# A fused attention and bilinear-GLU block on one core: where the weight totals and the attention steps stand in the joint down projection of chunks 0 and 1

## The chip, the cores and the metric

The kernel runs on one core of one Trainium2 chip. The metric is the device time of one execution in microseconds (us); the median of the runs counts. The profile was taken from one such execution and has a span of 772.1 us, from the first instruction to the last.

The engines are named as the profile names them: PE is the matmul engine (PEld its weight loads), DVE the vector engine, ACT the scalar engine, POOL the general-purpose engine. SPq is the queue from which the sync engine issues most transfers. Each engine works through its own list of instructions in the order of the program; a semaphore makes it wait where an operand comes from another engine or from a transfer.

## What is computed

The input is 2048 rows of 1024 bf16 numbers. The block is a layernorm, a sliding-window attention, an output projection with a residual, a second layernorm, and a feed-forward part without a nonlinear function, again with a residual:

```python
h  = x + attention(layernorm(x), wqkv) @ wo        # 32 heads, 8 keys each, two rows apart
n  = layernorm(h)
h2 = h + ((n @ w_gate) * (n @ w_up)) @ w_down      # w_gate, w_up: 1024 x 3584, w_down: 3584 x 1024
```

The kernel works in four chunks of 512 rows. The change lies in one stage: the last product, `@ w_down`, of chunks 0 and 1 together.

## The kernel before

**The joint product.** The activations `g * u` of chunks 0 and 1 and the weight `w_down` are seen as 2 x 2 blocks: A11 and A12 are chunk 0 (even and odd blocks of 128 hidden features), A21 and A22 chunk 1; B11, B12, B21, B22 are the even and odd row blocks of `w_down`, left and right halves of its columns. Seven block products in place of eight give the four blocks of the result (a Strassen-Winograd scheme). It needs sums and differences of blocks, which are made in fp16. So activations and weights are first multiplied by a power of two each, taken from a bound: the sum of absolute values of every row, the total over all partitions, its exponent. `scale_h1` is the one for the activations, `scale_d` the one for the weights.

```python
class Scale:
    def add(self, k, src, junk):          # ACT: |src| summed along the row into column k of l1
        nc.scalar.activation(junk, src, ACTF.Abs, accum_out=self.l1[:, k:k + 1])
    def rows(self):                       # DVE: one number for each partition, and it in bf16
        nc.vector.tensor_reduce(row[:], self.l1[:], ..., ALU.add)      # profile: L639
        nc.vector.tensor_copy(self.rowb[:], row[:])                    # profile: L640
    def total(self, ps=None):             # PE sums over partitions, DVE makes the scales
        nc.tensor.matmul(ps[:, 0:n], lhsT=ones[:], rhs=self.rowb[:]...)  # profile: L645
        nc.vector.tensor_copy(tot[:], ps[:, 0:1])                      # L647
        ...                                # eb, eb, sb, ib: four DVE instructions on one column, L649 to L654
```

A product of the stage is 14 matmuls for each of four groups of 128 rows:

```python
def dprod(ps, q, lhs, rhs, fresh, lo=0, n=TC):
    for k in range(NP):                                                # NP = 14, profile: L944
        nc.tensor.matmul(ps[:, bass.ds(lo, n)], lhsT=lhs[k][:, bass.ts(q, 128)], rhs=..., ...)
```

**Loads and helpers.** `load_down` brings one half of a B block (two transfers of 896 KB); `load_h1` brings A21 or A22 back from device memory, to which chunk 1's activations were written (`hd1`), in two transfers of 1024 and 768 KB. `conv_h1`, `conv_down` and `conv_a` multiply a block by its power of two into fp16, on DVE unless ACT is named. `s1_half` is A21 + A22 for one half, `t_half(d, x, y, a)` is a difference of two B blocks for one half, `put` adds the residual to a finished result and stores it, `seed` copies one accumulator, scaled, into another (ACT). `pull(1)` issues the next step of the attention of chunk 3, which still runs on DVE meanwhile: an operation on 128 x 4096 elements or a pair of them.

**The stage.** Cut to the lines that matter:

```python
b12 = halves(((att, "qD"), (att, "kD")), "b12")
load_down(b12, 0, 1)
a21 = ...; a22 = ...
load_h1(a21, 0)
load_h1(a22, 1)
...
# output projection of chunk 2 on PE; ACT sums |B11| and |B21| beside it (abs_blocks, tiles junkb)
wo_adds(2, {0: in_turn(lambda: pull(1), lambda: abs_blocks(b11 + b21)), ...})
xs = four accumulators "ex";  ys = four accumulators "ey"

for q in range(4):
    dprod(xs[q], q, A11, cells_of(b11, NH), True)          # A11 B11, still in bf16
    if q == 0:
        conv_h1(a21, 0)
        conv_h1(a22, 0)
        s1_half(0)
        scale_d.rows()
    if q == 1:
        pull(1)
        conv_h1(a21, 1, nc.scalar)
        conv_h1(a22, 1, nc.scalar)
    if q == 2:
        scale_d.total(ys[3])
        inv1 = ...                                          # one DVE instruction
        for i in range(3):
            seed(i)                                         # ys[i] = xs[i] * scale_d.s
seed(3)
for q in range(4):
    ys[q] = ys[q] * scale_h1.s                              # ACT
pull(1)
s1_half(1)
b22 = ...; load_down(b22, 1, 1)
FS1 = A21 + A22
conv_a(A11, F11, 0, NP); conv_down(b22, nc.scalar)          # ACT
for q in range(4):
    dprod(xs[q], q, A12, cells_of(b21, NH), False)          # A12 B21 on top, still in bf16
    put(0, q, 0, ...)
    if q < 2:
        conv_down([b11[q], b12[q]])
    if q > 0:
        t_half(b11, b12, b11, q - 1) if q < 3 else None     # B12 - B11
conv_a(A12, F12, 0, NP)
...
for q in range(4):
    ev = ...
    dprod(ev, q, FS1, fcells(b11), True)                    # (A21 + A22)(B12 - B11)
    ...
    s_sums(F11, FS1, F11, ALU.subtract, ...)                # 14 small DVE differences in all
    if q > 1:
        t_half(t2, b22, b11, q - 2)                         # B22 - (B12 - B11)
pull(2)
...
for q in range(4):
    dprod(ys[q], q, F11, fcells(t2), False)
    ...
    s_sums(F12, F12, F11, ALU.subtract, ...)
    pull(1)
```

Of the kernel before, what the change touches and what calls it, by code (L numbers as in the profile page):

```python
# [78 lines left out]
def kernel(  # L79
# [11 lines left out]
    nc = tc.nc  # L91
# [565 lines left out]
    scale_gu, scale_d, scale_h = Scale("gu", 28), Scale("d", 23), Scale("h", 56)  # L657
# [125 lines left out]
    def put(c, t, hf, dst, ps, sc, other):  # L783
        nc.vector.scalar_tensor_tensor(dst, ps[:], sc, other, ALU.mult, ALU.add)
        nc.sync.dma_start(outf[bass.ds(c * TC + t * 128, 128), bass.ts(hf, 512)], dst)
# [132 lines left out]
    def f16(ap):  # L918
        return ap.bitcast(F16)

    def to_f16(dst, src, sc, eng=nc.vector):
        if eng is nc.scalar:
            nc.scalar.activation(dst, src, ACTF.Copy, scale=sc)
        else:
            eng.tensor_scalar(dst, src, sc, None, ALU.mult)

    def load_down(homes, e, hf):
        for a, t in enumerate(homes):
            nc.sync.dma_start(t[:, 0:NH, :], wd_e[e][:, bass.ts(a, NH), bass.ts(hf, 512)])

    def conv_down(homes, eng=nc.vector):
        for t in homes:
            to_f16(f16(t[:, 0:NH, :]), t[:, 0:NH, :], scale_d.s, eng)

    def sub(dst, x0, x1, eng=nc.vector):
        for d, a0, a1 in zip(dst, x0, x1):
            eng.tensor_tensor(f16(d[:, 0:NH, :]), f16(a0[:, 0:NH, :]), f16(a1[:, 0:NH, :]), ALU.subtract)
# [4 lines left out]
    def dprod(ps, q, lhs, rhs, fresh, lo=0, n=TC):  # L942
        for k in range(NP):
            nc.tensor.matmul(ps[:, bass.ds(lo, n)], lhsT=lhs[k][:, bass.ts(q, 128)], rhs=rhs[k][:, bass.ds(lo, n)],  # L944
                             start=(fresh and k == 0), stop=(k == NP - 1), skip_group_check=not fresh)
# [13 lines left out]
    def pull(n):  # L959
        for _ in range(n):  # L960
            next(atts[3], None)

    b11, b21 = ([wts["dn", n, a] for a in range(2)] for n in ("11", "21"))

    def halves(parts, name):
        return [pool.tile([128, KO, TC], BF, tag=tag, name=f"{name}{i}") for i, (pool, tag) in enumerate(parts)]

    b12 = halves(((att, "qD"), (att, "kD")), "b12")
    load_down(b12, 0, 1)
    a21 = halves(((lnTp, "lnT"), (lnTp, "lnT")), "a21")  # L970
    a22 = halves(((lnTp, "lnT"), (wpool, "w")), "a22")

    def load_h1(dst, e, parts=(0, 1)):
        for i in parts:
            t, k, n = ((dst[0], 0, 8), (dst[1], 8, 6))[i]
            nc.sync.dma_start(t[:, 0:n, :], hd1[:, 2 * k + e:2 * (k + n):2, :])

    load_h1(a21, 0)
    load_h1(a22, 1)
    state["live"] += 1  # L980

    def cells_of(homes, n=8):
        return [t[:, k, :] for t in homes for k in range(n)][0:NP]
# [55 lines left out]
    def s1_half(i):  # L1039
        n = (8, 6)[i]  # L1040
        s, t = (f16(a[i][:, 0:n, :]) for a in (a21, a22))
        nc.vector.tensor_tensor(s, s, t, ALU.add)

    def conv_h1(a, i, eng=nc.vector):
        n = (8, 6)[i]
        to_f16(f16(a[i][:, 0:n, :]), a[i][:, 0:n, :], scale_h1.s, eng)

    def t_half(dst, x0, x1, a):
        sub([dst[a]], [x0[a]], [x1[a]])

    def conv_a(cells, fcells_, lo, hi):
        for k in range(lo, hi):
            to_f16(fcells_[k], cells[k], scale_h1.s, nc.scalar)
# [12 lines left out]
    def seed(q):  # L1066
        nc.scalar.activation(ys[q][:], xs[q][:], ACTF.Copy, scale=scale_d.s)

    for q in range(4):
        dprod(xs[q], q, A11, cells_of(b11, NH), True)  # L1070
        if q == 0:
            conv_h1(a21, 0)
            conv_h1(a22, 0)
            s1_half(0)
            scale_d.rows()
        if q == 1:
            pull(1)
            conv_h1(a21, 1, nc.scalar)
            conv_h1(a22, 1, nc.scalar)
        if q == 2:  # L1080
            scale_d.total(ys[3])
            inv1 = const.tile([128, 1], F32, name="inv_h1d")
            nc.vector.tensor_tensor(inv1[:], scale_h1.inv, scale_d.inv, ALU.mult)
            inv1 = inv1[:]
            for i in range(3):
                seed(i)
    seed(3)
    for q in range(4):
        nc.scalar.activation(ys[q][:], ys[q][:], ACTF.Copy, scale=scale_h1.s)
    pull(1)  # L1090
    s1_half(1)
    b22 = halves(((lnTp, "lnT"), (wpool, "w")), "b22")
    load_down(b22, 1, 1)
# [3 lines left out]
    for q in range(4):  # L1097
        dprod(xs[q], q, A12, cells_of(b21, NH), False)
        put(0, q, 0, hs0[q][:, 0:512], xs[q], 1.0, hs0[q][:, 0:512])
        if q < 2:  # L1100
            conv_down([b11[q], b12[q]])
        if q > 0:
            t_half(b11, b12, b11, q - 1) if q < 3 else None
    conv_a(A12, F12, 0, NP)
    retire(4)
    hss[3] = load_x(3, "h", nc.sync)
# [34 lines left out]
    a22 = halves(((att, "vD"), (att, "oD")), "a22r")  # L1141
# [212 lines left out]
```

## Time and profile before

| What | Value |
|---|---|
| Time, median of 3 runs (lowest to highest) | 774.48 us (773.71 to 774.75) |
| Span of the profiled execution (its time) | 772.1 us (774.36 us) |
| PE busy over the span | 764.2 us, 99% |
| DVE, ACT, POOL busy | 79%, 66%, 18% |
| 412.00 to 424.50 us: PE, DVE, ACT busy, of 12.50 us | 9.62, 10.27, 11.32 us |
| 424.50 to 440.15 us: PE, DVE, ACT busy, of 15.65 us | 15.47, 15.31, 13.87 us |
| 440.15 to 452.20 us: PE, DVE, ACT busy, of 12.05 us | 12.05, 12.05, 12.05 us |
| 452.20 to 476.60 us: PE, DVE, ACT busy, of 24.40 us | 24.40, 18.53, 13.71 us |
| Granted clock of PE | 1.00 throughout these stretches |

The times inside the span count from its first instruction. The stage of the change begins at 412.38 us, with the first matmul of A11 B11. In a line of the timeline the columns are: start, busy time of the merged group, engine, line of the kernel, operation, written tile and read tiles, shapes, count, and in square brackets the idle time of the engine just ahead of it with what ended it. The view of waits gives, for a waiting engine and the one that ended its wait, the total, the number of times and the longest. The profile's ends of matmuls are modelled; starts are what to count with.

### The profile page before, as it was taken

The numbers are of one execution on the slowest core, as the hardware profiler recorded it, in microseconds if no ns is written. First come the engines' busy times: TensorE is split into PE (matmuls) and PEld (weight loads), VectorE is DVE, ScalarE is ACT, GpSimd is POOL, SyncE is SP. The second block draws the span as 40 slices with busy tenths as digits, with TensorE's granted clock in tenths as the row PEclk, the third lists the DMA queues.
The fourth block names the chain that finished last, engine by engine and source line by source line (L and its number), as shares of the span: only waits on it lengthen the run. The fifth ranks groups of instructions, "written<-read, shape, count | busy, mean of one in ns | idle before, by whom it ended". The sixth has DMA issues, their size and how long they took to land.

```text
span 772.1 us, 10299 instructions
## 1 busy us (share of the span) xinstructions
PE 764.2 (99%) x3663; PEld 351.1 (45%) x3663; DVE 606.2 (79%) x718; ACT 513.4 (66%) x979; POOL 141.9 (18%) x152
## 2 busy tenths in 40 slices
PE   9999999999999999999998999999999999999998
PEld 6444444444444444444443444444444444444444
DVE  5639999999899999999998996985553444568863
ACT  4638966423687398777899985836677676788240
POOL 0000000200002000020000001008778687600000
DMA  8999796999957699489568357774332423740001
GB/s 276 267 264 247 228 259 142 299 292 288 308 190 235 215 284 308 145 264 315 185 210 273 125 188 239 144 178 107 97 106 59 110 65 100 247 135 28 0 28 54
DMA packets 190915, 144.85 MB, mean 188 GB/s; under 512 B 81808, under 2 KB 181136, under 8 KB 188688
## 3 DMA queue, kind: packets, MB, share of 16 engines
q1 hardware_dynamic: 180416, 116.94, 53.9%
q0 software_dynamic: 3584, 22.02, 8.3%
q10 hardware_dynamic: 6864, 5.24, 2.5%
q8 instruction: 28, 0.46, 0.3%
q14 instruction: 23, 0.19, 0.1%
HBM read 110.10 MB, written 27.26 MB: 178 GB/s over the span
## 4 chain that ended last, share of the span: by engine, by line
PE 75%; DVE 15%; ACT 4%; issue 3%; DMA 3%; ACTq 0%; DVEq 0%; SPq 0%
PE ps L431 21%; PE dx L944 6%; PE py L826 6%; PE px L826 6%; PE pz L826 6%; PE pu L431 4%; PE pg L431 4%; PE pv L826 3%; PE ez L944 3%; PE ey L944 3%; DVE pv L523 3%; PE dy L944 3%; DVE prod L477 2%; PE wo L998 2%; PE wo L602 2%
## 5 line engine op out<-in xcount | busy, mean ns | idle before, releaser
L431 PE MATMUL ps<-lnT,w_qkv 128*128 128x512 bf16 x736 | 159.5, 379 | 0.0
L431 PEld LDWEIGHTS <-w_qkv 128*128 128x128 bf16 x736 | 71.9, 98 | 86.1
L344 ACT CAST sg<-ps 128x512 bf16<-128x512 f32 x96 | 55.3, 586 | 47.6 <-PE ps L431 40.8
L477 DVE TENSOR_TENSOR prod<-qD,kD 128x4096 bf16<-128x4096 bf16 x32 | 72.2, 2285 | 12.4 <-DMA kD<-kd 12.4
L523 DVE TENSOR_TENSOR pv<-vD,at 128x4096 bf16<-128x4096 bf16 x32 | 72.4, 2285 | 0.2
L826 PEld LDWEIGHTS <-sw 128*128 128x128 f16 x448 | 43.8, 98 | 52.9 <-issue 0.2
L431 PEld LDWEIGHTS <-w_wu 128*128 128x128 bf16 x448 | 43.8, 98 | 52.9
L431 PEld LDWEIGHTS <-w_wg 128*128 128x128 bf16 x448 | 43.8, 98 | 52.9
L826 PE MATMUL px<-lnT,ws 128*128 128x512 bf16 x224 | 55.2, 379 | 0.0
L536 POOL DMA_DIRECT2D od<-oD x4 | 2.2, 544 | 276.7 <-DVE oD L534 276.7
L431 PE MATMUL pg<-lnT,w_wg 128*128 128x512 bf16 x224 | 52.9, 379 | 0.0
L431 PE MATMUL pu<-lnT,w_wu 128*128 128x512 bf16 x224 | 52.9, 379 | 0.0
L431 PE MATMUL pwu<-lnT,w_wu 128*128 128x512 bf16 x224 | 52.9, 379 | 0.0
L431 PE MATMUL pwg<-lnT,w_wg 128*128 128x512 bf16 x224 | 52.9, 379 | 0.0
L826 PEld LDWEIGHTS <-ws 128*128 128x128 f16 x336 | 32.9, 98 | 39.7
L807 POOL TENSOR_TENSOR sw<-ws 128x512 f16<-128x512 f16 x26 | 30.0, 1155 | 85.5 <-PE pv L826 51.9
L944 PEld LDWEIGHTS <-gs 128*128 128x128 f16 (+1 forms) x280 | 27.4, 98 | 36.4 <-issue 3.6
L479 DVE TENSOR_TENSOR prod<-prod 128x4096 bf16<-128x4096 bf16 x16 | 36.6, 2289 | 0.4
L843 ACT COPY py<-px 128x512 f32<-128x512 f32 x28 | 16.0, 570 | 27.8 <-PE px L826 27.8
L808 POOL TENSOR_TENSOR sw<-sw,ws 128x512 f16<-128x512 f16 x26 | 30.0, 1155 | 2.0
L810 POOL TENSOR_TENSOR sw<-ws,sw 128x512 f16<-128x512 f16 x26 | 30.0, 1155 | 0.0
L809 POOL TENSOR_TENSOR sw<-ws 128x512 f16<-128x512 f16 x26 | 30.0, 1155 | 0.0
(334 smaller groups left out, 1474.8 us busy)
## 6 DMA issues: line engine op xcount, KB each, us to landing
w_wg<-in_B_w_gate_dram SPq DMA_DIRECT2D x14, 1024.0 KB, 6.9
w_wu<-in_B_w_up_dram SPq DMA_DIRECT2D x14, 1024.0 KB, 6.3
w_pair<-in_B_w_gate_dram SPq DMA_DIRECT2D x14, 512.0 KB, 4.0
w_pair<-in_B_w_up_dram SPq DMA_DIRECT2D x14, 512.0 KB, 5.3
w_wo<-in_A_wo_dram SPq DMA_DIRECT2D x6, 1024.0 KB, 7.2
w_qkv<-in_A_wqkv_dram SPq DMA_DIRECT2D x5, 1024.0 KB, 10.9
kd<-sg SPq DMA_DIRECT2D x32, 144.0 KB, 4.2
kD<-kd POOLq DMA_DIRECT2D x4, 1152.0 KB, 9.0
```

Of the source, the lines that this page charges most:

```text
L344: nc.scalar.copy(sg[:, HB:HB + TC], ps[:])
L431: nc.tensor.matmul(ps[:], lhsT=wt[:, ko, bass.ts(j, 128)], rhs=rhs[:, ko, :], start=(ko == 0), stop=(ko == KO - 1))
L477: nc.vector.tensor_tensor(prod[:, j], qD[:], kD[:, :, o:o + SUB], ALU.mult)
L479: nc.vector.tensor_tensor(prod[:, :, 0:16], prod[:, :, 0:16], prod[:, :, 16:32], ALU.add)
L523: nc.vector.tensor_tensor(pv[:, j], vD[:, :, o:o + SUB], at[:, w, None, :].to_broadcast((128, DH, SUB)), ALU.mult)
L807: eng.tensor_tensor(sw[:, i, 0], a21, a22, ALU.add)
L808: eng.tensor_tensor(sw[:, i, 1], sw[:, i, 0], a11, ALU.subtract)
L809: eng.tensor_tensor(sw[:, i, 2], a11, a21, ALU.subtract)
L810: eng.tensor_tensor(sw[:, i, 3], a12, sw[:, i, 1], ALU.subtract)
L826: nc.tensor.matmul(ps[:], lhsT=lhs[:, ko, :], rhs=rhs[:, ko, :], start=(fresh and ko == 0), stop=(ko == 3), skip_group_check=not fresh)
L843: nc.scalar.copy(yb[i][:], xb[i][:])
L944: nc.tensor.matmul(ps[:, bass.ds(lo, n)], lhsT=lhs[k][:, bass.ts(q, 128)], rhs=rhs[k][:, bass.ds(lo, n)], start=(fresh and k == 0), stop=( ...
```

## The change: what it does and what it is for

The sum over rows of the weight bound (`scale_d.rows`) was placed on DVE behind two conversions and a sum of the A blocks; it now stands behind the first conversion alone, so that the total over partitions, a matmul in the middle of A11 B11, finds its operand earlier. The rest fills DVE in another order: the sum `s1_half(0)` comes behind the total; the weight conversions stand in one block right behind it instead of between the products of A12 B21; each weight difference is one step earlier in that loop; two attention steps move from ahead of the weight work to behind it. On ACT the second conversion of A22 comes behind the first three seeds. On the transfer queue the loads of A21 and A22 go ahead of that of B12. No instruction is added or taken away.

```diff
     b12 = halves(((att, "qD"), (att, "kD")), "b12")
-    load_down(b12, 0, 1)
     ...
     load_h1(a21, 0)
     load_h1(a22, 1)
+    load_down(b12, 0, 1)
     ...
         dprod(xs[q], q, A11, cells_of(b11, NH), True)
         if q == 0:
             conv_h1(a21, 0)
+            scale_d.rows()
             conv_h1(a22, 0)
-            s1_half(0)
-            scale_d.rows()
         if q == 1:
-            pull(1)
             conv_h1(a21, 1, nc.scalar)
-            conv_h1(a22, 1, nc.scalar)
         if q == 2:
             scale_d.total(ys[3])
             ...
+            s1_half(0)
             for i in range(3):
                 seed(i)
+            conv_h1(a22, 1, nc.scalar)
     seed(3)
     for q in range(4):
         nc.scalar.activation(ys[q][:], ys[q][:], ACTF.Copy, scale=scale_h1.s)
-    pull(1)
+    for a in range(2):
+        conv_down([b11[a], b12[a]])
     s1_half(1)
     ...
         put(0, q, 0, hs0[q][:, 0:512], xs[q], 1.0, hs0[q][:, 0:512])
         if q < 2:
-            conv_down([b11[q], b12[q]])
-        if q > 0:
-            t_half(b11, b12, b11, q - 1) if q < 3 else None
+            t_half(b11, b12, b11, q)
+        else:
+            pull(1)
```

## The prediction, written before the result was known

> **What bounds the kernel now.** The first line of the page says which engine to look at.
>
> ```profile
> PE 764.2 (99%) x3663; PEld 351.1 (45%) x3663; DVE 606.2 (79%) x718; ACT 513.4 (66%) x979; POOL 141.9 (18%) x152
> ```
>
> PE has only 772.1 - 764.2 = 7.9 us without a matmul. A reorder that adds and removes nothing can gain only from those. The view of waits, for PE alone, names them:
>
> ```profile
> PE ey L645 <- DVE rowbd L640: 2.9, 1, 2.9
> PE warm_ps L338 <- DVE warm L324: 1.2, 1, 1.2
> PE ps L392 <- ACT lnT L387: 0.4, 1, 0.4
> PE ps L392 <- DMA w_qkv<-in_A_wqkv_dram: 0.3, 1, 0.3
> PE ex L944 <- ACT ey L1067: 0.2, 1, 0.2
> ```
>
> The first and the last are of the changed stage; the rest belong to the start. L645 is the matmul that totals the weight bound over partitions. The PE timeline shows it in place:
>
> ```profile
> 412.38 9.23 PE L944 MATMUL ex<-w_dn,gs 128*128 128x512 bf16 x42
> 424.49 0.38 PE L645 MATMUL ey<-rowbd,ones 128*128 128x512 bf16 x1 [2.88 <-DVE rowbd L640]
> 424.70 3.18 PE L944 MATMUL ex<-w_dn,gs 128*128 128x512 bf16 x14
> 428.07 12.25 PE L944 MATMUL ex<-w_dn,gs 128*128 128x512 bf16 x56 [0.18 <-ACT ey L1067]
> 440.15 12.25 PE L944 MATMUL ev<-w_dn,a 128*128 128x512 f16 x56
> ```
>
> From 428.07 to 440.15 there are 56 matmuls: 12.08 / 56 = 215.7 ns from start to start. So PE was free for the total at 412.38 + 42 x 0.2157 = 421.44 and got it at 424.49: 3.05 us lost. After it, 14 matmuls should end their slots at 424.70 + 3.02 = 427.72, but the next started at 428.07: 0.35 lost. Together 3.40 us. The DVE timeline says why `rowbd` came late:
>
> ```profile
> 417.12 1.27 DVE L925 TENSOR_SCALAR a<-a,sbh 128x4096 f16<-128x4096 bf16 x1
> 420.55 1.29 DVE L925 TENSOR_SCALAR a<-a,sbh 128x4096 f16<-128x4096 bf16 x1 [2.16 <-DMA a<-hd]
> 421.87 2.29 DVE L1042 TENSOR_TENSOR a<-a,a 128x4096 f16<-128x4096 f16 x1
> 424.08 0.17 DVE L639 TENSOR_REDUCE rowd<-l1d 128x1 f32<-128x23 f32 x1
> 424.28 0.16 DVE L640 CAST rowbd<-rowd 128x1 bf16<-128x1 f32 x1
> 424.35 2.28 DVE L534 TENSOR_TENSOR oD<-oD,pv 128x4096 bf16<-128x4096 bf16 x1
> 426.55 0.15 DVE L647 COPY totd<-ey 128x1 f32<-128x1 f32 x1
> 427.18 0.14 DVE L654 TENSOR_SCALAR ibd<-ebd 128x1 int32<-128x1 int32 x1
> 446.81 3.95 DVE L937 TENSOR_TENSOR t<-b,w_dn 128x3584 f16<-128x3584 f16 x2
> ```
>
> The two row operations stand behind two conversions and a sum, and the second conversion waits 2.16 us for A22. Then an attention step of 2.28 us (L534) stands ahead of the copy of the total, so the scale is ready only near 427.3, and the first seed starts at 427.36 (the 0.18 above). On ACT the last summing of |B21| ended at 418.80: the rows could have been had from then on.
>
> [...] the trace has 2.28 us against 1.28 for 4096 columns, so the moved sums and attention steps are the long pieces.
>
> **The change, part by part.** I follow the new order with the durations above; on DVE I count from start to start, as operations overlap slightly there.
>
> *Rows.* DVE: first conversion 417.12 to 418.39, rows after ACT's 418.80, so about 419.0, bf16 copy done at 419.3. PE needs it at 421.44: slack 2.1. This takes away the 3.05, wherever A22 lands.
>
> *Total and seeds.* The second A22 half stays on ACT, but behind three seeds. The second DVE conversion runs 419.3 to 420.6 if A22 is there. The total starts on PE at 421.44, ends near 421.85; copy to `inv1` takes 427.44 - 426.55 = 0.89, so until 422.75. Seed 0 runs about 422.6 to 423.3; PE wants that accumulator at 421.44 + 0.21 + 3.02 = 424.67. Slack 1.4, so the 0.35 goes too. Seed 3 comes behind the conversion (seeds to 424.4, conversion 2.86 to 427.2, seed to 427.8), but PE needs it only after three more groups, at 424.67 + 9.06 = 433.7.
>
> *Loads.* Bytes and queue are the same; A21 and A22 (3.67 MB) pass B12 (1.84 MB). Before, A22's halves landed at about 420.5 and 422.7 (the two waits on them), at the end of some 5.5 MB. Now about B12's share, an estimated 1.84 MB / 350 GB/s = 5 us, is taken off their wait (350 GB/s is what the DMA view shows in these us), and B12 is last, near 422.7. Its first use is now at 422.75 + 2.21 (A sum) + 1.06 = 426.0: slack 3.
>
> *DVE, the part to worry about.* Its work up to the last weight difference is the same, but PE comes 3.4 us earlier. Before, from 420.55 to 450.68 DVE had 30.13 us with 0.28 idle, so 29.85 of work. Of this, conversion, rows and scale (1.32 + 0.27 + 0.89) lie ahead of 422.75 now. What is left is 27.37: two A sums 2.21 + 1.67, four weight conversions 4.24, four differences 3.87 + 3.87, four puts 2.41, two attention steps 4.40, 14 small differences 4.70. Sum: 422.75 + 27.37 = 450.1. Its points against PE:
>
> First difference B12 - B11: 422.75 + 2.21 + 4.24 + 1.67 + 0.60 + 1.94 = 433.4; PE starts `ev` at 424.67 + 12.08 = 436.75. The second: 433.4 + 0.60 + 1.94 = 435.95 against 436.75 + 7 x 0.2157 = 438.3. Both have over 2 us, where before the second ended at 441.6 for a need of 441.66. This is what moving the attention steps is for.
>
> Then attention and puts to 441.55, small differences to 446.25, B22 - (B12 - B11): first half 448.2, second 450.1 to 450.2. PE ends `ev` at 436.75 + 12.09 = 448.84 and needs the second half at 448.84 + 1.51 = 450.35. Slack 0.6 and about 0.15: just in time, so an expected loss of 0.1, up to 1 if some DVE piece waits.
>
> *Further on.* Differences for A12 end some 0.6 earlier than before (461.5 for 462.1); the last is needed at 460.9 + 2.8 = 463.7. DVE had an idle 4.77 us after these, so its debt ends there. The last attention output ends at about 458.2 and its transfers some 13 us later (before: 458.75, landed by 472.4); PE wants it from 473.1 on, before from 476.41. Slack remains. From there each later step hangs on PE and shifts with it.
>
> Sum: 3.05 + 0.35 - 0.1 = 3.3 us. 774.48 - 3.3 = 771.2.
>
> **The rivals.**
>
> *DVE becomes the bound.* PE's wait would not vanish but move to the start of `ey`, on L937 (t). For it: from 424.5 to 452.2 DVE is busy 27.36 of 27.70 us, and by my count 0.15 us remains. Against it: DVE begins the scale 4.7 us earlier (421.86 for 426.55), as the 2.16 us wait is gone and two attention steps moved. If DVE loses 1 to 2 us to a wait that I don't see, the time is 772 to 773.
>
> *B12 lands too late.* It is now last in the queue. DVE would wait at its conversion, and through the tight chain each us would arrive at PE, less 0.15. For it: three of four A loads issue with long gaps, and A21's second half must wait for chunk 1's last store. Against it: 3 us of slack. At 2 us late it costs nothing; at 5 us late, 773.
>
> *The gain is absorbed later*, by something that doesn't move with PE: the way of chunk 3's attention through device memory. Its slack falls from some 4 us to some 1.3 (landed 471.8, last rows) or more, as the first rows are used first. If it were to fail, up to 3 us come back: 774.
>
> *Nothing to gain* would need the PE wait to be hidden. A wait on an engine that is 99% busy and on the chain is not; I give this little.
>
> **Range and chances.** Centre 771.2. Medians of three of the same kernel lie in 773.71 to 774.75, half a us each way. Below, no more than the 3.4 can come from this stage, so 770.3 is the end with noise. Above, I allow 1.3 us for the tight DVE chain and noise: 772.6. 2% of 774.48 is 15.5 us; PE's whole idle time is half of that, so "faster by over 2%" is all but excluded, and so is the reverse, as the order is only changed inside some 40 us with PE near full in both.
>
> **What would show it right or wrong.** Right: no PE wait on `rowbd`; the total at about 421.4 and A12 B21 at 424.7, `ev` at 436.8, `ey` at 448.8, the output projection of chunk 3 at 473.1; PE's busy time unchanged and the span near 768.8. The DVE conversion of A22 without a DMA wait; L937 of t ending within 0.3 us of 450.2. Wrong: a PE wait on L937 (t) at `ey`, or on L1112; a DVE wait on B12; a wait of the output projection on oT; or a later wait that takes back the 3.3 us.

## The result: 770.39 us for 774.62, and the profile after

The changed kernel takes 770.39 us (median of 6 runs, 770.02 to 770.98), the kernel before on the same chip 774.62 us (6 runs, 773.71 to 775.11). The ratio is 0.9948, with a 95% interval of 0.9935 to 0.9960: 4.2 us faster, inside 2%. The predicted time was 771.2 with a range of 770.3 to 772.6.

The waits of PE, changed kernel (who waited for whom, total, times, longest):

```profile
PE warm_ps L338 <- DVE warm L324: 1.2, 1, 1.2
PE pt L386 <- DVE ln L379: 0.8, 1, 0.8
PE ps L392 <- DMA w_qkv<-in_A_wqkv_dram: 0.5, 1, 0.5
PE ps L392 <- ACT lnT L387: 0.3, 1, 0.3
```

All four belong to the start of the kernel. The waits on `rowbd` and on the seed are gone and nothing took their place. The PE timeline, changed kernel:

```profile
412.41 9.23 PE L944 MATMUL ex<-w_dn,gs 128*128 128x512 bf16 x42
421.48 0.38 PE L645 MATMUL ey<-rowbd,ones 128*128 128x512 bf16 x1
421.69 15.27 PE L944 MATMUL ex<-w_dn,gs 128*128 128x512 bf16 x70
436.80 12.25 PE L944 MATMUL ev<-w_dn,a 128*128 128x512 f16 x56
448.89 12.25 PE L944 MATMUL ey<-t,gs 128*128 128x512 f16 x56
```

A11 B11 and A12 B21 have become one group of 70 without a gap. From the first matmul of `ex` to the first of `ey<-t` there are 42 + 1 + 14 + 56 + 56 = 169 slots; 169 x 0.2157 = 36.45 us, and the trace has 448.89 - 412.41 = 36.48. I call this span the stage length. It is now where PE alone would put it, with no wait left. In the kernel before it was 452.24 - 412.38 = 39.86, from the line of 412.38 in the prediction to this one of the same timeline:

```profile
452.24 12.25 PE L944 MATMUL ey<-t,gs 128*128 128x512 f16 x56
```

The DVE timeline, changed kernel, at the two places that mattered:

```profile
418.86 0.18 DVE L639 TENSOR_REDUCE rowd<-l1d 128x1 f32<-128x23 f32 x1 [0.43 <-ACT junkb L635]
419.15 1.28 DVE L925 TENSOR_SCALAR a<-a,sbh 128x4096 f16<-128x4096 bf16 x1
421.89 0.16 DVE L647 COPY totd<-ey 128x1 f32<-128x1 f32 x1 [1.46 <-PE ey L645]
446.27 3.95 DVE L937 TENSOR_TENSOR t<-b,w_dn 128x3584 f16<-128x3584 f16 x2
```

The row sums wait for nothing but the last sum on ACT; A22 is there when its conversion comes (no wait on the line at 419.15, where 2.16 us stood before); DVE now waits for PE, 1.46 us, in place of the reverse. The differences t end at 450.22, 0.18 us ahead of PE's need for the second half at 448.89 + 1.51 = 450.40.

The traces explain 772.1 - 768.7 = 3.4 us of span. The times differ by 4.2. The rest is settled below.

### The profile page after: what moved, and what is told of

It is laid out like the page before. It is cut to its first block, busy times and chain, and to the rows that moved or that the text cites. A ratio compares the mean times of both kernels' runs of the same rounds, so it can differ in the third digit from the quotient of the medians.

```text
span 768.7 us, 10302 instructions
## 1 busy us (share of the span) xinstructions
PE 762.8 (99%) x3663; PEld 350.7 (46%) x3663; DVE 606.0 (79%) x718; ACT 513.1 (67%) x979; POOL 142.5 (19%) x152
## 4 chain that ended last, share of the span: by engine, by line
PE 97%; DVE 2%; DMA 1%; issue 0%; ACTq 0%; DVEq 0%
PE ps L431 21%; PE dx L944 6%; PE pz L826 6%; PE pwu L431 6%; PE pu L431 6%; PE py L826 6%; PE pwg L431 6%; PE pg L431 6%; PE px L826 6%; PE wo L998 4%; PE pv L826 3%; PE ez L944 3%; PE ey L944 3%; PE ex L944 3%; PE dy L944 3%; PE wo L578 2%
```

## The experiments

Times are medians; each ratio is against the kernel before on the same chip, with its 95% interval, and is the recorded estimate, not the quotient of the medians shown. Not all rows ran on the same chip. The stage length is the sharper measure, as it is read inside one trace. Where a line of a trace has x41, x55 or x69, one record is missing: the starts fit 42, 56 and 70.

| Kernel | Stage length, us | Time, us | Ratio to before |
|---|---|---|---|
| before | 39.86 | 774.62 | |
| changed | 36.48 | 770.39 | 0.9948 (0.9935 to 0.9960) |
| row sums moved alone | 39.66 | 774.53 | 0.9996 (0.9986 to 1.0007) |
| row sums and total moved | 39.40 | 773.50 | 0.9987 (0.9980 to 0.9993) |
| the same, and ACT's conversion behind the seeds | 39.40 | 773.58 | 0.9986 (0.9977 to 0.9995) |
| changed, old loads | 36.47 | 770.61 | 0.9949 (0.9934 to 0.9964) |
| changed, row sums second | 36.47 | 770.63 | 0.9950 (0.9935 to 0.9964) |
| changed, both of these | 37.07 | 771.14 | 0.9951 (0.9939 to 0.9963) |
| changed, ACT's conversion ahead of the seeds | 36.66 | 770.90 | 0.9941 (0.9927 to 0.9955) |
| the same, old loads | 37.73 | 772.16 | 0.9956 (0.9942 to 0.9970) |
| changed, attention step later | 36.47 | 770.75 | 0.9954 (0.9939 to 0.9968) |
| changed, one DVE operation more | 37.88, and one more wait behind it | 772.76 | 0.9969 (0.9958 to 0.9980) |
| changed, again | 36.47 | 771.00 | 0.9948 (0.9937 to 0.9960) |

**Row sums moved alone**, the edit in the kernel before:

```diff
             conv_h1(a21, 0)
+            scale_d.rows()
             conv_h1(a22, 0)
             s1_half(0)
-            scale_d.rows()
```

> The kernel before with one edit: the row sums of the weight bound stand behind the first conversion of A21, as in the changed kernel; loads, attention steps and conversions stay. Theory 1 (a wait moves on): PE gets the total at about 421.5 us and loses nothing there, but the copy of the total still stands on DVE behind the A22 conversion (held by its load until 420.5), the A sum and an attention step, so the scale is ready at about 427.1 us; A12 B21 then waits some 3.1 us for the first seed and starts near 427.9 instead of 428.07. Gain 0.2 us, time same as before. Rival (the row sums are the gain, as the title of the change says): the 2.9 us wait just goes, gain about 3 us.

The PE timeline, row sums moved alone:

```profile
421.99 0.38 PE L645 MATMUL ey<-rowbd,ones 128*128 128x512 bf16 x1
422.20 3.19 PE L944 MATMUL ex<-w_dn,gs 128*128 128x512 bf16 x14
428.42 12.25 PE L944 MATMUL ex<-w_dn,gs 128*128 128x512 bf16 x55 [3.03 <-ACT ey L1067]
```

DVE took its operations in the order of the program both times: the row sums ran at 424.08 in the kernel before and at 419.36 here, ahead of the conversion that waits for A22 (420.55 and 421.16). The total runs without a wait, and one product later PE waits 3.03 us for the seed. The stage is 0.20 us shorter, as expected. A wait of 2.88 us on one line is not 2.88 us of gain: behind it stood a second wait with the same end.

**Row sums and total moved**: the A sum and the attention step that stood ahead of the total go behind it too.

```diff
             conv_h1(a21, 0)
+            scale_d.rows()
             conv_h1(a22, 0)
-            s1_half(0)
-            scale_d.rows()
         if q == 1:
-            pull(1)
             ...
             inv1 = inv1[:]
+            s1_half(0)
+            pull(1)
```

> The kernel before with the row sums moved forward and the A sum and the attention step that stood ahead of the total moved behind it; the attention steps stay ahead of the weight differences, and the loads stay in the old order. Theory 1: A12 B21 starts at 424.7 us (3.4 us gained), but the first weight difference ends at about 438.5 us where the next product wants it at 436.8 (wait 1.7), the second at 441.0 where it is wanted at 440.0 (wait 1.0): gain left 0.7 us. Rival (DVE has room enough for the attention steps where they were): gain 3.4 us.

The PE timeline, row sums and total moved:

```profile
425.88 12.25 PE L944 MATMUL ex<-w_dn,gs 128*128 128x512 bf16 x55 [1.19 <-ACT ey L1067]
438.51 1.67 PE L944 MATMUL ev<-w_dn,a 128*128 128x512 f16 x7 [0.39 <-DVE w_dn L937]
441.05 10.74 PE L944 MATMUL ev<-w_dn,a 128*128 128x512 f16 x49 [0.86 <-DVE w_dn L937]
```

The stage gains 0.46 us, where 0.7 was expected. The weight differences hold PE back, though by 1.3 us in all and not by 2.7, since the wait of 1.19 us for the seed, which was not foreseen, came ahead of them. Two runs follow it up.

**ACT's second A22 conversion put back ahead of the seeds**, in the changed kernel, with the new and with the old order of the loads:

```diff
             conv_h1(a21, 1, nc.scalar)
+            conv_h1(a22, 1, nc.scalar)
         ...
             for i in range(3):
                 seed(i)
-            conv_h1(a22, 1, nc.scalar)
```

> The changed kernel with ACT's second A22 conversion put back ahead of the seeds; loads in the new order. The run with row sums and total moved showed a wait of 1.2 us for the first seed that was not expected there, with that conversion ahead of the seeds and A22 loaded last. Theory 1 (the place of this conversion counts, and the more the later A22 lands): with A22 landed early ACT converts 421.5 to 424.35 us, the first seed ends at about 425.0, PE wants it at 424.7: wait 0.3 us, time 0.3 above the changed kernel. Rival (the conversion's place costs nothing): no wait.

> The same with the loads in the old order too. Theory 1: the conversion waits for its load until some 422.3 to 422.7 us and ends near 425.3, the first seed ends at 426.0, PE waits 1.2 to 1.5 us; time 1.2 to 1.5 above the changed kernel. So the order of the loads is worth 1 us here and nothing where the conversion stands behind the seeds. Rival (the wait came from DVE, as the scale was late): no wait here, as the scale is at 422.7 us.

The ACT timeline of the second, with old loads:

```profile
422.77 2.86 ACT L923 ACTIVATE a<-a,sbh 128x3072 f16<-128x3072 bf16 x1 [0.95 <-DMA a<-hd]
425.54 2.38 ACT L1067 ACTIVATE ey<-ex,sbd 128x512 f32<-128x512 f32 x4
```

The scale was ready at 423.0, but ACT held the seeds until 425.54, as the conversion ahead of them waited for A22. PE lost 1.25 us of stage length. With the new order of the loads the same placing costs 0.19 us (0.3 expected). So the early A22 load takes away all but 0.19 us of this wait, and the conversion behind the seeds takes away all of it, with either order of the loads.

**The attention steps and the weight conversions**: the run above with row sums and total moved, and in addition ACT's conversion behind three seeds. Against the changed kernel only the attention steps, the weight conversions with the differences behind them, and the loads stand as before. The edit in the changed kernel, without the loads:

```diff
             s1_half(0)
+            pull(1)
             for i in range(3):
                 seed(i)
     ...
-    for a in range(2):
-        conv_down([b11[a], b12[a]])
+    pull(1)
     s1_half(1)
     ...
         if q < 2:
-            t_half(b11, b12, b11, q)
-        else:
-            pull(1)
+            conv_down([b11[q], b12[q]])
+        if q > 0:
+            t_half(b11, b12, b11, q - 1) if q < 3 else None
```

> The run with row sums and total moved, with ACT's second A22 conversion behind three seeds: against the changed kernel only the attention steps and the weight conversions stand in their old order (and the loads, which the run with old loads showed to cost nothing). Theory 1: A12 B21 starts without a wait at 424.7 us, and all of the loss now stands at the weight differences: PE waits 1.7 us for the first and 0.9 to 1.0 for the second; time as in the run with the conversion ahead, to 0.2 us, since DVE set it there too; 2.6 us above the changed kernel. Rival (half the loss there was ACT's): 1.2 us faster than that run.

The PE timeline, attention ahead:

```profile
421.73 15.27 PE L944 MATMUL ex<-w_dn,gs 128*128 128x512 bf16 x69
438.74 1.67 PE L944 MATMUL ev<-w_dn,a 128*128 128x512 f16 x7 [1.74 <-DVE w_dn L937]
441.28 10.73 PE L944 MATMUL ev<-w_dn,a 128*128 128x512 f16 x49 [0.86 <-DVE w_dn L937]
```

No wait for the seed any more, and the stage is exactly as long as with it, 39.40 us: DVE's weight differences set the end in both. The old order of attention steps and conversions costs 39.40 - 36.48 = 2.92 us (2.6 expected), of the 3.38 that the whole change brings in this stage. This is the largest part. The two steps take 4.5 us on DVE here, 425.03 to 429.56, ahead of work that PE waits for. But the conversions were not tried alone, and the 2.92 belong to the pair: with the steps away and the conversions still between the products, DVE would be done with the A sum near 425.03 + 1.67 = 426.70 and could not take the first finished product before 421.73 + 2 x 3.02 = 427.77, an estimated idle time of 1 us where, as shown below, only some 0.2 us can be spared. What moving the steps would bring with the total still late is open too.

**Loads and row sums**, undone one at a time and together in the changed kernel.

```diff
+    load_down(b12, 0, 1)                  # old loads
     ...
-    load_down(b12, 0, 1)
     ...
-            scale_d.rows()                # row sums second
             conv_h1(a22, 0)
+            scale_d.rows()
```

> The changed kernel with the loads in the order of the kernel before (B12 ahead of A21 and A22). Theory 1 (the order of the loads is worth nothing while the row sums stand ahead of the A22 conversion): that conversion waits for its load until about 420.5 us and ends at 421.85, when the total arrives from PE (421.86 to 421.9): PE timeline as in the changed kernel to 0.1 us, same time. Rival (the early A22 is part of the gain): the total is late and PE waits 0.5 us or more, or the load of B22 and B12 shifts a DVE wait.

> The changed kernel with the row sums behind both DVE conversions. Theory 1 (with A22 loaded early the place of the row sums is worth nothing): the second conversion runs right behind the first, 418.4 to 419.6 us, the row sums are done at about 419.9, still 1.5 us ahead of PE's need at 421.5: no PE wait, same time as the changed kernel. Rival (the place of the row sums is the gain): a PE wait for them comes back and 1 us or more is lost.

> The changed kernel with both undone: loads in the old order and the row sums behind both conversions. Theory 1 (the two are substitutes; undone together they cost): the A22 conversion is held until 420.5 us, the row sums are done at about 422.1, PE waits 0.6 to 0.8 us for them; the second DVE half of the stage shifts by as much and adds nothing. Time 0.7 us above the changed kernel. Rival (each is worth something alone, or neither): no wait of PE, or over 1.5 us lost.

Each alone costs nothing (36.47), both together 0.59 us of stage length, where 0.7 was expected. The medians show only 771.14 - 771.00 = 0.14, the mean spans 769.4 - 768.8 = 0.6. The DVE timeline with both undone:

```profile
420.85 1.29 DVE L925 TENSOR_SCALAR a<-a,sbh 128x4096 f16<-128x4096 bf16 x1 [2.03 <-DMA a<-hd]
422.05 0.17 DVE L639 TENSOR_REDUCE rowd<-l1d 128x1 f32<-128x23 f32 x1
422.26 0.16 DVE L640 CAST rowbd<-rowd 128x1 bf16<-128x1 f32 x1
```

The row sums end at 422.4 where PE was free for them at 421.9. They are substitutes: either the row sums don't stand behind the load, or the load is early. The row sums named first in the change are not where the time came from, once the loads are reordered.

**How full DVE is.** One operation more, and one less, ahead of the small differences in the changed kernel:

```diff
             t_half(b11, b12, b11, q)
         else:
             pull(1)
+    spare = f16(b12[0][:, 0:NH, :])                              # one operation more
+    nc.vector.tensor_tensor(spare, spare, spare, ALU.max)
```

```diff
-        else:
+        elif q == 2:
             pull(1)                                              # attention step later
     ...
-    pull(2)
+    pull(3)
```

> The changed kernel with one more DVE operation of 2.0 us (B12's first half, maximum with itself, in place, so that nothing in the result changes) behind the last attention step ahead of the small differences. Theory 1 (DVE is full here and the slack at the product behind is 0.2 to 0.6 us): the differences t end 2 us later, PE waits about 1.4 us for the first and in sum 1.7 to 1.8 us for both; time 1.7 to 1.8 us above the changed kernel, as nothing later gives it back. Rival (there is room on DVE): same time.

> The changed kernel with one of the two attention steps moved from ahead of the small differences to behind the differences t. Theory 1 (PE waits nowhere in this stage any more): t ends 2.2 us earlier, slack on DVE grows to about 2.4 us, the attention output ends where it did, and PE's timeline does not change; same time. Rival (the tight chain costs PE something that the profile doesn't name): up to 0.5 us faster.

The PE timeline, one operation more:

```profile
450.36 1.68 PE L944 MATMUL ey<-t,gs 128*128 128x512 f16 x7 [1.23 <-DVE t L937]
452.29 10.74 PE L944 MATMUL ey<-t,gs 128*128 128x512 f16 x49 [0.25 <-DVE t L937]
```

Of 1.93 us that the operation takes on DVE, 772.76 - 771.00 = 1.76 reach the time of the kernel, and nothing later gives them back. So the slack is near 0.2 us, as the trace said. The step later left the stage at 36.47 and the time the same (770.75 against 771.00): with no wait of PE there is nothing to win. (Its profile shows 774.3 us, as that one execution had a wait of 4.4 us for a transposed tile early in the kernel; the others lay at 768.5 to 769.2. More on it below.)

**The changed kernel and the kernel before again**, for the open 0.8 us:

> The changed kernel itself again, on the chip of the three others: the reference for their differences. By the trace 3.4 us below the kernel before; the first comparison had 4.2 us, with an interval that holds both. Theory 1: the 3.4 us is all, and the difference comes out between 3.2 and 4.2. Rival: another 0.8 us is gained outside the stage, and 4.2 comes again, with spans that are 4 us apart.

> The kernel before, profiled once more. Its spans over 52 runs gather near 771.9 and near 773.2 us, while those of the changed kernel gather near 768.7 alone. Theory A: the 1.2 us between the two is a later landing of A22, which stands on the path of the kernel before and not on that of the changed one; a profile with a span near 773.2 then shows the DVE wait for A22 near 3.4 instead of 2.16 us and the total's matmul wait near 4.1 instead of 2.9. Theory B: it is at the start of the kernel (PE waits within the first 30 us) and the stage itself is as before. A profile with a span near 772 tells nothing.

The comparison gave 4.2 us in the first set of runs and 4.0 in the second (774.97 - 771.00). The second lies inside the range of the first theory, so the times don't decide. The spans do: over all sets the kernel before has a mean span of 772.85 us (84 executions) and the changed kernel 768.65 (11), which is 4.2 apart, as the rival had it. The spans of the kernel before come in two groups, and this time the profile (773.8 us) fell in the upper one. It shows neither theory A nor theory B. The DVE wait for A22 is 2.25 us and the total's wait 2.98, much as before, and the start of the kernel hardly differs. The PE timeline, kernel before again:

```profile
412.76 9.23 PE L944 MATMUL ex<-w_dn,gs 128*128 128x512 bf16 x41
424.96 0.58 PE L645 MATMUL ey<-rowbd,ones 128*128 128x512 bf16 x1 [2.98 <-DVE rowbd L640]
453.97 12.25 PE L944 MATMUL ey<-t,gs 128*128 128x512 f16 x56
```

The view by stages, kernel before again (stretch, its length, busy time of PE, PEld, DVE, ACT and POOL with counts, granted clock, share and rate of transfers):

```profile
421.40:425.00 3.60, 0.62 (x4) 0.22 (x3) 3.53 (x5) 2.34 (x2) 0.00 (x0) 0.97 0.02 7
425.00:426.00 1.00, 1.00 (x3) 0.37 (x3) 1.00 (x1) 1.00 (x1) 0.00 (x0) 0.50 0.30 33
427.00:428.00 1.00, 1.00 (x4) 0.39 (x3) 0.86 (x8) 0.17 (x1) 0.00 (x0) 0.50 1.09 360
428.00:429.00 1.00, 1.00 (x6) 0.42 (x5) 1.00 (x1) 1.00 (x3) 0.00 (x0) 0.89 0.72 249
```

The granted clock is 0.50 from 424.8, just ahead of PE's new start, to 428.2, for 3.4 us (both ends are estimates from the means of 0.97 and 0.89 in the stretches there): three or four matmuls are counted in a us, where five to seven are in the first profile of the same kernel, at 1.00. The weight loads of these matmuls start 427 ns apart (425.35 to 427.91, six steps), about twice the 215.7 ns between matmuls at 1.00. The stage length is 453.97 - 412.76 = 41.21 us, 1.35 more than in the first profile of the same kernel, whose clock stayed at 1.00. An estimate from these figures comes near: PE works 428.2 - 424.96 = 3.2 us at half clock, which costs 1.6, and the 0.35 that was lost to the seed falls into that time, which leaves some 1.3.

A mean clock of 0.996 to 0.998 was recorded in 53 of the 84 executions of the kernel before, all with spans of 772.8 us and more; the other 31 have 1.00 and spans of 771.4 to 772.3. None of the 11 of the changed kernel has it. The run with the row sums alone, which keeps a pause of 3.03 us, had it in 7 of 14. The runs whose longest pause in the stage was 1.1 to 1.7 us (row sums and total moved, attention ahead, ACT's conversion ahead with old loads, one DVE operation more) had it in none of 44. A mean of 0.999, in one execution each of three runs, is not counted: in the one of the row sums alone, the clock is 1.00 in every stretch from 412 to 442 us, the pause and what follows it among them.

One execution of the changed order has a lowered mean too: the profiled one of the run with the step later, which had the early pause of 4.4 us, has 0.998, and the nine others 1.00. Its stage begins at 417.92, where that of the changed kernel again began at 412.56: 5.4 us later, 1.0 more than the pause. The stage length of 36.47 shows that nothing was lost in the stage; where the clock fell was not shown. So in these records the drop goes with a pause of about 3 us or more. No run put such a pause into the changed kernel by itself.

By this estimate the pause costs its own length and, in some 63% of executions, 1.35 us more: 3.38 + 0.63 x 1.35 = 4.2 us on average, which is the difference of the mean spans. Two runs bear this out roughly: with row sums and total moved, and with attention ahead, the stage is only 0.46 shorter, but the long pause is gone; their mean spans are 1.1 and 1.0 us below those of the kernel before on the same chip.

## Why the prediction was right, and what it missed

The steps, against the trace of the changed kernel:

- *Rows*: total at 421.4 predicted, 421.48 measured; the bf16 copy done at 419.23 for 419.3. Right, and the runs on loads and row sums bear out "wherever A22 lands".
- *Total and seeds*: A12 B21 without a wait, at 421.69 + 3.02 = 424.71 for 424.67; the three seeds from 422.71 on. Right in its times. It gave the conversion's new place only as an order to follow, with no cost of the old one; the two runs put 0.19 us on it, or 1.25 with A22 late, and the seed wait was missing from the forecast of the run with row sums and total moved for that reason.
- *Loads*: A22 early and B12 without a wait of DVE. Right. That the new order of the loads is worth nothing beside the other parts was measured (36.47).
- *DVE*: `ev` at 436.80 for 436.75, `ey` at 448.89 for 448.84, t done at 450.22 for 450.1 to 450.2. The slack of 0.15 us was 0.18. On 4096 columns the tensor-tensor operation took 2.28 us again and the one-source conversion 1.28. The rival "DVE becomes the bound" did not come true, but by 0.2 us only; the run with one operation more shows it from the other side.
- *Further on*: output projection of chunk 3 at 473.06 for 473.1, no wait there; span 768.7 for 768.8. The gain was not absorbed.

What failed is the sum, "3.05 + 0.35 - 0.1 = 3.3", and with it the statement that a reorder "can gain only from" the time without a matmul. The sum lacks a term: what a pause of 3 us did to the clock of the matmuls behind it, an estimated 0.63 x 1.35 = 0.85 us on average. The prediction took the 215.7 ns between matmuls for fixed, on one trace, in which the clock stayed at 1.00; that they stay so behind a pause was its author's assumption. In the trace with the drop the weight loads started 427 ns apart, at a clock of 0.50. The half clock lasted 3.4 us there, though PE worked for only 3.2 us of that. The pause ahead of it was 2.98 us by the profile's idle time, while pauses of 2.88 and 3.03 us in two other traces left the clock at 1.00. The expected loss of 0.1 on DVE did not occur either. Both errors made the forecast too high by 0.95 us, less 0.14 as the kernel before took 774.62 this time and not 774.48: 0.8. The low end of the range, 770.3, rested on "no more than the 3.4 can come from this stage" and on noise. The gain went beyond that, and that 770.39 still fell inside, by 0.09 us, is luck.

## What to carry to other kernels

A wait in a list is worth what stands behind it: moving the row sums took away 2.9 us of wait and won 0.2, because the seed ended almost as late; with the seed freed as well, the weight differences took back most of the gain. Follow the released engine to its next need, and the one after, before counting a gain. Where an engine that isn't the bound is nearly full, as DVE was here with 0.18 us to spare, the order in which it works decides (2.92 us here): the steps that no one waits for soon belong behind those that are needed next.

## What the hardware did that was not expected

A pause of PE went on costing after it ended. In one trace, with a pause of 2.98 us, the granted clock fell to 0.50 at an estimated 424.8 us, while PE still stood (until 424.96), and stayed there for 3.4 us; in two others, with pauses of 2.88 and 3.03 us, it stayed at 1.00. By the mean clock of each execution, it fell in 53 of 84 of the kernel before, 7 of 14 with the row sums moved, and none of 44 with pauses of 1.1 to 1.7 us; in the one execution with a pause of 4.4 us, early in the kernel, the mean was 0.998. In the stage, the drop that was traced cost 1.35 us beside the pause. What decides from run to run was not tried.
